# Scans of the next chunk ordered behind the masks of the present one on VectorE

## The chip, the cores and the metric

The kernel runs on one core of a Trainium2 chip. The metric is the time of one execution on the device in microseconds (us), the median of three runs. TensorE (PE) does the matrix products, VectorE (DVE), ScalarE (ACT) and GpSimd (POOL) the element-wise work, and SyncE (SP) issues all transfers from one queue. Each engine works through its own list of instructions in order and waits on semaphores.

## The reference

Three parts follow one another: a linear attention with decay, and two feed-forward layers.

```python
for t in range(S):                      # S = 768, for 4 batches and 8 heads of width 48
    state = alpha[:, :, t, :, None] * state + einsum('bhd,bhe->bhde', k[:, :, t], v[:, :, t])
    y[:, :, t] = einsum('bhd,bhde->bhe', q[:, :, t], state)
...
x = y as 3072 tokens x 384
h = x @ w_in;  x = (h * sigmoid(1.702 * h)) @ w_out      # 384 -> 2048 -> 384
h = x @ w_in2; x = (h - tanh(h)) @ w_out2
```

## The kernel before

The sequence of each batch is cut into six chunks of 128 tokens, so there are 24 chunks, counted here from 0. Within a chunk the recurrence becomes products. VectorE makes running products of the decays by two scans (`a_scan`: a memset of four columns, a scan, a reciprocal, a second scan). The keys and queries are scaled with them (`a_scale`, on GpSimd from chunk 8 on). TensorE makes the scores (`a_whole`, L298), VectorE masks them into SBUF in two halves (L301), and TensorE makes the output of a chunk in `a_out`: the queries times the carried state (L325) and the masked scores times the values (L332), both into the banks in which the scores were, and the chunk's own addition to the state (L341), which needs the keys turned by sixteen 32-row transposes on VectorE (`a_turn`, L308). `a_state` (L352, L353) then adds that to the state and multiplies it with the decays of the next chunk. `a_guard` (L254) squares the decays of a chunk in place on ScalarE, for a check at the end; the buffer of these decays is free for a load only after it. Results go to memory (`a_evac`: copies on ScalarE, L360, and four stores), come back turned (`a_back`, L378), and are split into a high and a low part (`a_x`: L382 on ScalarE, L383 on VectorE, the tile `xlo`). There are two sets of chunk buffers, so chunk g + 2 is loaded where chunk g was: the decays by L232, the keys by L234, the queries by L236, the values by L238.

The feed-forward layers run over six blocks of 512 tokens each, and over 16 slices m of the 2048 wide middle. Of each step TensorE makes nine products of the first kind (L392) and, three steps later, nine of the second (L399). In between ScalarE applies the function (L406) and rounds the result (L409, `ghi`), and VectorE makes the rest (L410, `glo`). `evac` (L442, L445) takes a finished block out. In the first layer's steps of block j the attention of the four chunks of block j + 1 is worked in small parts between the steps: `attend(g, r)` for the parts r = 0 to 3 of chunk g. Chunks 8 to 23 fall into blocks 1 to 4, some 135 to 450 us of the span; from chunk 8 (`FULL`) on a chunk's eight heads are worked at once. In blocks 2 and 3 weights are loaded a second time (L156) and checked on VectorE and ScalarE (`w_check`, L170 and L172), and towards the end of block 4 the second layer's weights are converted on VectorE (L163, L164, L176).

What sets the order: the lists of the engines are made by a scheduler of the language from the program, its dependencies and priorities. Only the first block's steps are held in the order written (`in_order`). After that the scheduler may move an instruction ahead of others that were written earlier, where no dependency forbids it. The masks carry a high priority. In the kernel before, the scans of chunk g + 1 are written ahead of the masks of chunk g.

Of the kernel before, what the change touches and what calls it, by code (L numbers as in the profile page):

```python
# [13 lines left out]
ALU = mybir.AluOpType  # L14
# [3 lines left out]
C = 128  # L18

FULL = 8  # L20
NCH = S // C
NG = B * NCH
NP = H // 2
# [45 lines left out]
def linear_attention_mlps(ctx, tc, xq, xv, fa, fv, cst, w1, w2, out):  # L69
    nc = tc.nc  # L70
    V, A, G, P, SP = nc.vector, nc.scalar, nc.gpsimd, nc.tensor, nc.sync
# [32 lines left out]
    ident, mask = cs[:, 0:128], cs[:, 128:256]  # L104
    seg = T("seg", (DP, AW))
    first = seg.rearrange("p (h t) -> p h t", h=NP)[:, :, 0:1]
# [92 lines left out]
    def src(g, n):  # L199
        return (third if g == 2 else late[(g + (g > 2)) % 2])[n][: DP if n < 4 else 128]  # L200

    def dec(g, n):
        return src(g, n)
# [4 lines left out]
    def dec3(g, n):  # L208
        return pairs(dec(g, n))


    def qq(g):
        return dec3(g, 2)

    def qkk(g):
        return dec3(g, 3)
# [20 lines left out]
        if 4 in parts:  # L237
            SP.dma_start(out=src(g, 4), in_=xv[g])  # L238

    def a_scan(g, n):  # L240
        if n == 0:
            V.memset(first, 1.0)
        V.tensor_tensor_scan(out=dec(g, n), data0=src(g, n), data1=seg, initial=0.0, op0=ALU.mult, op1=ALU.max)  # L243
        if n == 0:
            V.reciprocal(out=first, in_=dec3(g, 0)[:, :, C:])
# [26 lines left out]
    def a_scores(g, x, b):  # L272
        u = (2 * g + x) % 2
        q, k = qq(g), qkk(g)
        o = [bank[b + hh][:, : 2 * CE].rearrange("p (a t) -> p a t", a=2) for hh in range(2)]
        for i in range(2):
            for hh in range(2):
                r = slice(64 * hh, 64 * hh + D)
                P.matmul(out=o[hh][:, i], lhsT=k[r, 2 * x + i], rhs=q[r, 2 * x + i], start=True, stop=True)
        s4 = sm[u].rearrange("p (b a t) -> p b a t", b=2, a=2)  # L280
        kt = kts[u].rearrange("p (b a t) -> p b a t", b=2, a=2)
        for hh in range(2):
            A.copy(s4[:, hh], o[hh][:, :, :C])
        s3 = sm[u].rearrange("p (a t) -> p a t", a=4)
        G.affine_select(out=s3, in_=s3, pattern=[[0, 4], [1, C]], channel_multiplier=1, base=1 - C,
                        compare_op=ALU.is_ge, fill=0.0)
        for hh in range(2):
            A.copy(kt[:, hh], o[hh][:, :, C:])


    def a_whole(g, b):
        q, k = qq(g), qkk(g)
        s8 = sm8.rearrange("p (b a t) -> p b a t", b=2, a=NP)
        o = [bank[b + hh].rearrange("p (a t) -> p a t", a=NP) for hh in range(2)]
        for p in range(NP):
            for hh in range(2):
                r = slice(64 * hh, 64 * hh + D)
                P.matmul(out=o[hh][:, p], lhsT=k[r, p], rhs=q[r, p, :C], start=True, stop=True)  # L298
        for hh in range(2):
            with tc.high_priority():  # L300
                V.tensor_tensor(out=s8[:, hh], in0=o[hh], in1=mask.unsqueeze(1).to_broadcast([128, NP, C]), op=ALU.mult)  # L301

    def a_turn(g, low):
        k = pairs(late[(g + (g > 2)) % 2][3])
        for x in (0, 2) if low else (1, 3):
            d = kt8[g % 2][:, 4 * D * (x // 2) + 32 * (x % 2) :][:, : NP * D].rearrange("p (a d) -> p a d", a=NP)[:, :, :32]
            for y in range(4):
                V.transpose(out=d[32 * y : 32 * y + 32], in_=k[32 * x : 32 * x + 32, :, 32 * y : 32 * y + 32])  # L308
# [177 lines left out]
    def prep(g, part):  # L486
        if g >= NG:
            return
        if part < 2:
            a_scan(g, part)  # L490
        if part == 2:
            a_scale(g)
        if part == 3:
            a_guard(g)

    def a_done(g, b=5):
        a_evac(g, b)
        if g + 2 < NG:
            a_load(g + 2)
        if g < FULL:  # L500
            a_back(g)

    def attend(g, r, b=5):
        if r == 0:
            prep(g + 1, 0)
        if g < FULL and r < 2:
            a_scores(g, r, b)
        elif r == 0:
            if g == FULL:
                a_turn(g, 0)  # L510
            a_whole(g, b)
            a_turn(g, 1)
        if r == 2:
            a_out(g, b)
        if 0 < r < 3 or r == 3 and g >= FULL:
            prep(g + 1, r)
        if r == 3 and g >= FULL:
            a_done(g, b)
            if g + 1 < NG:
                a_turn(g + 1, 0)  # L520
# [69 lines left out]
    def place(s):  # L590
        l, j, m = steps[s]
        i = j if l == 1 else len(L1) + j
        t0, n = (L1 if l == 1 else L2)[j]
        alt = i >= len(L1) - 1 and (i - len(L1)) % 2
        return l, j, m, i, t0, n, [bank[b] for b in ((5, 6, 7) if alt else (0, 1, 2))]

    for s in range(NS + LAG):
        if s:
            if s <= NS:
                l, j, m, i, t0, n, acc = place(s - 1)  # L600
                prev = s - 1, n, V
        if s < NS:
            l, j, m, i, t0, n, acc = place(s)
# [13 lines left out]
        if s < NS:  # L617
            if l == 1 and j + 1 < len(L1):
                t1, n1 = L1[j + 1]
                if j:  # L620
                    parts, span = n1 // C * 4, 11
                    todo = range(min(parts, -(-m * parts // span)), min(parts, -(-(m + 1) * parts // span)))
                else:
                    todo = ((4 * (m // 3) + m % 3,) if m % 3 < 2 else (4 * (m // 3) + 2, 4 * (m // 3) + 3)) if m < 12 else ()
                for r in todo:
                    attend(t1 // C + r // 4, r % 4)
# [35 lines left out]
        if s >= LAG:  # L662
            l, j, m, i, t0, n, acc = place(s - LAG)
# [8 lines left out]
    with tc.If(bad != 0):  # L672
# [3 lines left out]
        for i in range(B * NP):  # L676
            b, p = divmod(i, NP)
# [96 lines left out]
```

## Time and profile before

| | |
|---|---|
| median of three runs | 953.47 us (952.26 to 953.66) |
| the profiled execution | 957.78 us, its span from first to last instruction 956.1 us |
| TensorE busy | 913.8 us, 96% of the span |
| VectorE busy | 676.5 us, 71% |
| ScalarE busy | 449.5 us, 47% |
| GpSimd busy | 85.9 us, 9% |
| mean granted clock of TensorE | 0.988 |

A busy TensorE here means that products follow one another without a gap; the end of a product is modelled. The busy share of the other engines says little, since each of them waits for TensorE most of the time. The idle time of an engine is listed with the instruction that ended it, as "[idle before <-what released it]".

### The profile page before, as it was taken

The numbers are of one execution on the slowest core, as the hardware profiler recorded it, in microseconds if no ns is written. First come the engines' busy times: TensorE is split into PE (matmuls) and PEld (weight loads), VectorE is DVE, ScalarE is ACT, GpSimd is POOL, SyncE is SP. The second block draws the span as 40 slices with busy tenths as digits, with TensorE's granted clock in tenths as the row PEclk, the third lists the DMA queues.
The fourth block names the chain that finished last, engine by engine and source line by source line (L and its number), as shares of the span: only waits on it lengthen the run. The fifth ranks groups of instructions, "written<-read, shape, count | busy, mean of one in ns | idle before, by whom it ended". The sixth has DMA issues, their size and how long they took to land.

```text
span 956.1 us, 13257 instructions
## 1 busy us (share of the span) xinstructions
PE 913.8 (96%) x4870; PEld 728.1 (76%) x4870; DVE 676.5 (71%) x1124; ACT 449.5 (47%) x906; POOL 85.9 (9%) x70
## 2 busy tenths in 40 slices
PE   5569999999989999999999999999999999999997
PEld 4347777777768777777888888888888888888885
DVE  7799997844774787484159986766776777766663
ACT  4445533323434434343344564554566566544542
POOL 1201211101120111110100200100100001000000
PEclk9999999989989999999999999999999999999999
DMA  9767434422643565434125410200322420000001
GB/s 268 236 201 240 137 87 125 120 68 79 200 132 141 159 196 198 128 113 158 32 93 181 138 60 1 78 22 1 113 96 89 166 99 1 33 1 1 34 1 37
DMA packets 58107, 101.91 MB, mean 107 GB/s; under 512 B 5024, under 2 KB 37408, under 8 KB 58032
## 3 DMA queue, kind: packets, MB, share of 16 engines
q1 hardware_dynamic: 58032, 100.97, 33.7%
q8 instruction: 40, 0.66, 0.3%
q14 instruction: 35, 0.29, 0.1%
HBM read 86.79 MB, written 14.16 MB: 106 GB/s over the span
## 4 chain that ended last, share of the span: by engine, by line
PE 61%; DVE 0%; issue 0%; ACT 0%; ACTq 0%
PE bank L399 30%; PE bank L392 29%; PE bank L332 1%; PE bank L298 0%; PE bank L325 0%; PE bank L341 0%; DVE xs L442 0%; DVE arena L301 0%; PE bank L268 0%; ACT xs L445 0%; ACTq L671 0%
## 5 line engine op out<-in xcount | busy, mean ns | idle before, releaser
L410 DVE TENSOR_TENSOR glo<-gt,ghi 128x512 fp32r<-128x512 f32 x192 | 140.1, 732 | 151.0 <-ACT ghi L409 146.8
L392 PE MATMUL bank<-xhi,whi 128*128 128x512 f32 x576 | 229.2, 398 | 9.5 <-ACT xhi L382 8.8
L399 PE MATMUL bank<-ghi,whi 128*128 128x512 f32 x576 | 233.1, 405 | 0.0
L399 PE MATMUL bank<-ghi,wlo 128*128 128x512 f32 x576 | 229.0, 397 | 0.0
L392 PE MATMUL bank<-xlo,whi 128*128 128x512 f32 x576 | 228.5, 397 | 0.4 <-DVE xlo L383 0.4
L399 PE MATMUL bank<-glo,whi 128*128 128x512 f32 x576 | 228.5, 397 | 0.0
L392 PE MATMUL bank<-xhi,wlo 128*128 128x512 f32 x576 | 228.1, 396 | 0.0
L409 ACT CAST ghi<-gt 128x512 fp32r<-128x512 f32 x192 | 119.2, 621 | 220.8 <-DVE gt L421 133.1
L392 PEld LDWEIGHTS bank<-xhi,whi 128*128 128x128 f32 x576 | 109.2, 190 | 35.6 <-ACT xhi L382 9.0
L399 PEld LDWEIGHTS bank<-ghi,whi 128*128 128x128 f32 x576 | 109.2, 190 | 28.4 <-issue 1.9
L392 PEld LDWEIGHTS bank<-xlo,whi 128*128 128x128 f32 x576 | 109.3, 190 | 26.4 <-DVE xlo L383 1.2
L399 PEld LDWEIGHTS bank<-glo,whi 128*128 128x128 f32 x576 | 109.4, 190 | 25.7
L392 PEld LDWEIGHTS bank<-xhi,wlo 128*128 128x128 f32 x576 | 109.1, 189 | 25.5
L399 PEld LDWEIGHTS bank<-ghi,wlo 128*128 128x128 f32 x576 | 109.5, 190 | 24.2 <-issue 0.5
L406 ACT ACTIVATE gt<-bank 128x512 f32<-128x512 f32 x96 | 57.4, 597 | 95.6 <-PE bank L392 72.0
L308 DVE STREAM_TRANSPOSE cf<-arena 32x128 f32<-32x128 f32 x256 | 77.5, 303 | 24.9 <-PE bank L341 10.0
L419 DVE SCALAR_TENSOR_TENSOR arena<-arena,bank 128x512 f32<-128x512 f32 x96 | 65.8, 686 | 29.4 <-ACT arena L417 28.6
L421 DVE SCALAR_TENSOR_TENSOR gt<-arena 128x512 f32<-128x512 f32 x96 | 68.3, 712 | 10.9 <-DVE arena L420 1.4
L417 ACT ACTIVATE arena<-bank 128x512 f32<-128x512 f32 x96 | 57.3, 597 | 36.1 <-PE bank L392 35.7
L243 DVE TENSOR_TENSOR_SCAN arena<-arena,seg 112x516 f32<-112x516 f32 x46 | 63.5, 1380 | 14.6 <-DMA arena<-xq 13.6
L418 ACT ACTIVATE arena<-arena,cs 128x512 f32<-128x512 f32 x96 | 69.6, 725 | 2.9
L420 DVE SCALAR_TENSOR_TENSOR arena<-arena 128x512 f32<-128x512 f32 x96 | 67.9, 707 | 3.0
(89 smaller groups left out, 663.2 us busy)
## 6 DMA issues: line engine op xcount, KB each, us to landing
raw<-w SPq DMA_DIRECT2D x64, 768.0 KB, 4.5
arena<-xq SPq DMA_DIRECT2D x46, 224.0 KB, 4.4
arena<-xq SPq DMA_DIRECT2D x22, 451.5 KB, 5.1
xlo<-xt SPq DMA_DIRECT2D x24, 192.0 KB, 4.4
x1t<-xs SPq DMA_DIRECT2D x6, 768.0 KB, 3.4
arena<-x1t SPq DMA_DIRECT2D x6, 768.0 KB, 4.5
out<-xs SPq DMA_DIRECT2D x18, 256.0 KB, 2.3
arena<-xv SPq DMA_DIRECT2D x23, 192.0 KB, 3.3
```

The costliest lines, as they stand in the source:

```text
L243: V.tensor_tensor_scan(out=dec(g, n), data0=src(g, n), data1=seg, initial=0.0, op0=ALU.mult, op1=ALU.max)
L308: V.transpose(out=d[32 * y : 32 * y + 32], in_=k[32 * x : 32 * x + 32, :, 32 * y : 32 * y + 32])
L392: P.matmul(out=h, lhsT=w[m][:, ws], rhs=x[:, k, :n], start=c == 0, stop=c == 3 * KT - 1)
L399: P.matmul(out=acc[k][:, :n], lhsT=w[m][:, ws], rhs=x[s % 3][:, :n], start=m == 0 and c == 0, stop=m == MT - 1 and c == 2)
L406: A.activation(out=gf[i][:, :n], in_=h, func=AF.Silu, scale=1.702)
L409: A.copy(ghi[s % 3][:, :n], gf[s % 2][:, :n])
L410: e.tensor_tensor(out=glo[s % 3][:, :n], in0=gf[s % 2][:, :n], in1=ghi[s % 3][:, :n].bitcast(F32), op=ALU.subtract)
L417: A.activation(out=u, in_=h, func=AF.Square, accum_out=usum[:, s - NS1 :][:, :1])
L418: A.activation(out=w, in_=u, func=AF.Square, bias=pbias)
L419: V.scalar_tensor_tensor(out=p, in0=u, scalar=P3, in1=h, op0=ALU.mult, op1=ALU.mult)
L420: V.scalar_tensor_tensor(out=p, in0=u, scalar=-PR, in1=p, op0=ALU.add, op1=ALU.mult)
L421: V.scalar_tensor_tensor(out=gf[i], in0=w, scalar=PD, in1=p, op0=ALU.add, op1=ALU.mult)
```

## The change

The scan of the next chunk is no longer called at the head of `attend` for chunks from 8 on. It is called after `a_whole`, and its first instruction, the memset, is ordered behind the second mask by a dependency that sets the order in the list and needs no semaphore, since both are on VectorE. For the chunks before 8 all stays as it was.

```diff
-    def a_scan(g, n):
+    def a_scan(g, n, after=None):
         if n == 0:
-            V.memset(first, 1.0)
+            ins = V.memset(first, 1.0).ins
+            if after:
+                tc.add_manual_dep(ins, after, mybir.DependencyInfo(
+                    mybir.DependencyClass.NoSync, mybir.DependencyReason.DATA), reason="masks")
         V.tensor_tensor_scan(out=dec(g, n), data0=src(g, n), data1=seg, initial=0.0, op0=ALU.mult, op1=ALU.max)
...
         for hh in range(2):
             with tc.high_priority():
-                V.tensor_tensor(out=s8[:, hh], in0=o[hh], in1=mask.unsqueeze(1).to_broadcast([128, NP, C]), op=ALU.mult)
+                last = V.tensor_tensor(out=s8[:, hh], in0=o[hh], in1=mask.unsqueeze(1).to_broadcast([128, NP, C]), op=ALU.mult)
+        return last.ins.name
...
     def attend(g, r, b=5):
-        if r == 0:
+        if r == 0 and g < FULL:
             prep(g + 1, 0)
         if g < FULL and r < 2:
             a_scores(g, r, b)
         elif r == 0:
             if g == FULL:
                 a_turn(g, 0)
-            a_whole(g, b)
+            masks = a_whole(g, b)
+            if g + 1 < NG:
+                a_scan(g + 1, 0, masks)
             a_turn(g, 1)
```

With the scans the scheduler moves other instructions too. The lines of the changed kernel are 3 to 6 higher: the masks are L304, the transposes L312, the state L356 and L357, `xlo` L387, the copy back L382, `glo` L414, `ghi` L413, the guard L257.

On VectorE, the rows up to chunk 11's masks in the kernel before (the scans of the chunks after it, L243, stand ahead of the two masks, L301):

```order
L308 STREAM_TRANSPOSE cf_100<-arena 32x4x32 x7
L410 TENSOR_TENSOR glo_112<-gt,ghi_109 128x512
L383 TENSOR_TENSOR xlo_105<-xlo_105,xhi_103 128x3x128
L410 TENSOR_TENSOR glo_113<-gt,ghi_110 128x512
L243 SCALAR_TENSOR_TENSOR arena<-arena,seg 112x516
L245 RECIPROCAL seg<-arena 112x4
L243 SCALAR_TENSOR_TENSOR arena<-arena,seg 112x516
L242 MEMSET seg 112x4
L243 SCALAR_TENSOR_TENSOR arena<-arena,seg 112x516
L301 TENSOR_TENSOR arena<-bank_128,cs 128x512
L301 TENSOR_TENSOR arena<-bank_129,cs 128x512
```

In the changed kernel, VectorE's rows around chunk 10's masks, from the transposes of chunk 10 to the first scan of chunk 11:

```order
L312 STREAM_TRANSPOSE cf_100<-arena 32x4x32 x16
L414 TENSOR_TENSOR glo_112<-gt,ghi_109 128x512
L356 TENSOR_TENSOR state<-bank_130,state 112x192
L357 TENSOR_TENSOR state<-state,arena 112x192
L414 TENSOR_TENSOR glo_113<-gt,ghi_110 128x512
L304 TENSOR_TENSOR arena<-bank_128,cs 128x512
L387 TENSOR_TENSOR xlo_105<-xlo_105,xhi_103 128x3x128
L304 TENSOR_TENSOR arena<-bank_129,cs 128x512
L242 MEMSET seg 112x4
L246 SCALAR_TENSOR_TENSOR arena<-arena,seg 112x516
```

The scans stand behind the masks, the transposes of a chunk stand between its scans and its masks and ahead of the state, and at this place the `xlo` of chunk 9 has come between the two masks of chunk 10.

On SP, in the kernel before, from the stores of chunk 9's result on (L365 the stores, L238 values, L378 the copy back, L232 decays, L234 keys):

```order
L365 DMA xt<-arena 48x2x128 x4
L238 DMA arena<-xv 128x384
L378 DMA xlo_105<-xt 128x3x128
L232 DMA arena<-xq 112x1032
L234 DMA arena<-xq 112x512
```

The same place in the changed kernel:

```order
L369 DMA xt<-arena 48x2x128 x4
L238 DMA arena<-xv 128x384
L232 DMA arena<-xq 112x1032
L382 DMA xlo_105<-xt 128x3x128
L234 DMA arena<-xq 112x512
```

The load of decays and the copy back have changed places; the same holds for chunks 8, 10 and 20. The third place is SP's list between the copy back of chunk 16 and the weight loads of the checks, in the changed kernel:

```order
L382 DMA xlo_105<-xt 128x3x128
L232 DMA arena<-xq 112x1032
L234 DMA arena<-xq 112x512
L453 DMA x1t<-xs 128x3x512
L232 DMA arena<-xq 112x1032
L236 DMA arena<-xq 112x4x128
L238 DMA arena<-xv 128x384
L369 DMA xt<-arena 48x2x128 x4
L156 DMA raw_96<-w 128x1536
L156 DMA raw_97<-w 128x1536
```

Before, both loads of decays (of chunks 19 and 20) stood together ahead of the load of keys, and the values ahead of the stores, as here. On ScalarE, the guard of a chunk stood behind the next `ghi` (chunks 9 and 10), and now stands ahead of it, directly behind the evacuation of the chunk before.

## Rows read from the trace of the kernel before

**Rows 1.** The page's first part: engine, busy us, share of span, instructions.
```profile
PE 913.8 (96%) x4870; PEld 728.1 (76%) x4870; DVE 676.5 (71%) x1124; ACT 449.5 (47%) x906; POOL 85.9 (9%) x70
```

**Rows 2.** TensorE's waits, 180 to 520 us: total, times, longest.
```profile
PE bank L325 <- DVE arena L301: 5.2, 5, 3.0
```

**Rows 3.** Timeline of TensorE: start, us, engine, line, operation [idle before <-releaser].
```profile
191.35 0.42 PE L325 MATMUL bank<-arena,state 48*48 48x128 f32 x4 [1.45 <-DVE arena L301]
191.95 1.09 PE L325 MATMUL bank<-arena,state 48*48 48x128 f32 x12 [0.18 <-DVE arena L301]
...
277.98 1.69 PE L325 MATMUL bank<-arena,state 48*48 48x128 f32 x16 [3.04 <-DVE arena L301]
```

**Rows 4.** Windows: us, busy PE PEld DVE ACT POOL, granted clock, DMA, GB/s.
```profile
191.80:198.60 6.80, 6.65 (x37) 5.14 (x38) 6.19 (x19) 1.36 (x3) 1.19 (x1) 0.51 0.38 100
277.10:283.90 6.80, 5.92 (x47) 4.70 (x48) 3.74 (x11) 0.74 (x2) 2.24 (x2) 0.51 0.22 57
```

**Rows 5.** Timeline of VectorE ahead of chunk 11's and chunk 15's masks.
```profile
188.45 2.27 DVE L243 TENSOR_TENSOR_SCAN arena<-arena,seg 112x516 f32<-112x516 f32 x1
190.64 1.26 DVE L301 TENSOR_TENSOR arena<-bank,cs 128x512 f32<-128x512 f32 x2
...
274.48 1.23 DVE L243 TENSOR_TENSOR_SCAN arena<-arena,seg 112x516 f32<-112x516 f32 x1 [1.52 <-DMA arena<-xq]
...
277.24 0.68 DVE L301 TENSOR_TENSOR arena<-bank,cs 128x512 f32<-128x512 f32 x1
```

**Rows 6.** Timeline of TensorE: scores of chunk 8, state products of 9 and 10.
```profile
139.20 1.16 PE L298 MATMUL bank<-arena 48*128 48x128 f32 x16
...
160.89 0.66 PE L325 MATMUL bank<-arena,state 48*48 48x128 f32 x16
...
173.01 0.66 PE L325 MATMUL bank<-arena,state 48*48 48x128 f32 x16
```

**Rows 7.** Timeline of VectorE, chunks 8 to 10: what its instructions take.
```profile
147.65 2.65 DVE L308 STREAM_TRANSPOSE cf<-arena 32x128 f32<-32x128 f32 x8
150.24 0.30 DVE L353 TENSOR_TENSOR state<-state,arena 112x192 f32<-112x192 f32 x1
...
152.91 0.69 DVE L410 TENSOR_TENSOR glo<-gt,ghi 128x512 fp32r<-128x512 f32 x1
...
157.55 0.67 DVE L442 TENSOR_SCALAR xs<-bank 128x512 f32<-128x512 f32 x1
...
174.06 2.24 DVE L243 TENSOR_TENSOR_SCAN arena<-arena,seg 112x516 f32<-112x516 f32 x1
```

**Rows 8.** Timeline of GpSimd beside the last of these.
```profile
174.03 1.18 POOL L249 TENSOR_TENSOR arena<-arena 112x512 f32<-112x512 f32 x1 [8.17 <-DVE seg L245]
```

**Rows 9.** Timeline of ScalarE: a cast of ghi, guard of 9, xhi of 8.
```profile
149.06 0.62 ACT L409 CAST ghi<-gt 128x512 fp32r<-128x512 f32 x1 [1.94 <-PE bank L399]
150.62 1.06 ACT L254 ACTIVATE arena<-arena 112x1032 f32<-112x1032 f32 x1 [0.95 <-DVE state L353]
...
153.73 0.51 ACT L382 CAST xhi<-xlo 128x384 fp32r<-128x384 f32 x1 [1.47 <-DMA xlo<-xt]
```

**Rows 10.** Timeline of SP: back8, and the pair of weight loads.
```profile
150.04 0.40 SPq L378 DMA_DIRECT2D xlo<-xt  x1
...
338.52 0.92 SPq L156 DMA_DIRECT2D raw<-w  x2
```

**Rows 11.** Line 378, the copies back: from issue to landing.
```profile
DMA to landing us min/median/max: 2.5/4.4/6.3
```

**Rows 12.** Timeline of TensorE: scores of chunk 17, output of chunk 18.
```profile
324.43 1.16 PE L298 MATMUL bank<-arena 48*128 48x128 f32 x16
...
346.63 0.43 PE L332 MATMUL bank<-arena 128*48 128x128 f32 x4 [0.21 <-DVE arena L301]
```

**Rows 13.** Timeline of VectorE: the weight check ahead of chunk 18's masks.
```profile
345.41 0.56 DVE L170 TENSOR_SCALAR wtb<-raw 128x768 int16<-128x768 int16 x1 [0.41 <-DMA raw<-w]
```

**Rows 14.** Groups of VectorE by line: a weight conversion, busy us, mean ns.
```profile
L164 DVE SCALAR_TENSOR_TENSOR cf<-raw,cf 128x768 int32<-128x768 int32 x22 | 21.4, 972 | 0.7
```

## The prediction, made before the changed kernel ran

> **What bounds the kernel now.** The page comes first: TensorE is busy for 96% of the span [rows 1], and the chain that ended last is almost wholly its two big products. So an edit that only reorders VectorE can give or take nothing but time in which TensorE stands, and time in which it runs at the lower clock. The table of TensorE's waits, asked for the stretch in which whole chunks are worked (180 to 520 us), has one line of weight: the product with the carried state (L325) waits for the mask (L301), 5.2 us in five waits [rows 2]. The timeline shows the two that matter: 1.45 and 0.18 us at 191 us (chunk 11) and 3.04 us at 278 us (chunk 15) [rows 3]. Each has a second cost. In the 6.8 us that follow, the granted clock is 0.51, which is the 1.2 GHz level, against 2.4 GHz around them [rows 4]. Work done at half rate loses half of the stretch: 3.4 us after the first; after the second 6.8 less the 0.88 us still idle, halved, 3.0 us. With a wait of 0.21 at chunk 18 [rows 12], what the order of masks costs now is 5.2 + 0.2 + 3.4 + 3.0 = 11.8 us.
>
> The cause is on VectorE's timeline: just ahead of the late masks stand scans of later chunks [rows 5]. One of them sat 1.52 us for its own transfer; another took 2.27 us; the masks behind them then began at 190.64 and 277.24 us although their scores had long been there.
>
> **What the change removes.** In the new order the masks of a chunk come ahead of the next chunk's memset and scans at all fifteen places, so these two waits lose their cause. What is left ahead of chunk 11's masks is glo and xlo; ahead of chunk 15's its own transposes, the state, two glo and an xlo, which by the chain worked below end about 1 us before the product is due. I book the whole 11.8 us as removed. No instruction is added or dropped; the memset carries an order, not a semaphore.
>
> **What it adds.** Before, scans, scaling and transposes of a chunk ran a chunk ahead. Now they form a loop from mask to mask, and it must fit in the 12 to 16 us between two chunks' scores. I work it out for chunks 8 to 10, on the times of before, since little ahead of chunk 8's scores changes but that VectorE has less to do.
>
> Scores of 8 begin at 139.2 and take 1.16 [rows 6]: 140.4. Two masks, 1.26 [rows 5]: 141.7. First scan 1.23 [rows 5], reciprocal 0.2, second scan 2.24 because GpSimd multiplies beside it [rows 7, 8]: 145.4. One glo, 0.65 (its row has 0.69 [rows 7] and overlaps the next a little): 146.1. Sixteen transposes, 5.3 (eight take 2.65 [rows 7]): 151.4. State, two instructions of about 0.33 [rows 7]: 152.1. Now ScalarE: its guard, which squares the decays in place, waits for that state, as it did before [rows 9], and ScalarE's cast of ghi now stands behind the guard: 1.07 + 0.62 [rows 9], 153.8. Then glo 0.65 and masks of 9, until 155.8; no harm, they are due at 160.9 [rows 6].
>
> But SP has changed too. The load of chunk 11's decays, which waits for that guard, now stands ahead of the copy back of chunk 8 (back8). Back8 was issued at 150.04 [rows 10]; now it is issued after 153.4, at about 153.9. These copies land 2.5 to 6.3 us after issue [rows 11]; before, this one took 3.7 [rows 9, 10]. I take 3.8, since 451 KB of decays now go out just ahead of it: 157.7. Cast and xlo, 0.5 each: 158.8. Chunk 10's scan stands behind this xlo: 1.23, evacuation 0.67, reciprocal, glo 0.65 and scan [rows 5, 7] end at 163; transposes 168.4; glo and state 169.8; guard 170.9; ghi and glo 172.2; first mask 172.9. Then the place that decides: xlo9 stands **between the two masks of chunk 10**. Its copy back again waits on SP for guard and load: issued 171.4, landed 175.2, cast and xlo 176.3, second mask 176.9. The product with the state was due at 173.0 [rows 6].
>
> The late evacuation costs TensorE first: the next column block's middle product needs it at about 159.5 (six matmuls of 0.23 ahead of the 160.9), and it ends near 160.7 or, with landings of 2.5, at 159.4: 0 to 1.2, I take 0.6. The wait for the second mask is then 2.0 with landings of 2.5, which bring every later step forward by 1.3, to 3.5 with those of 3.8 and no shift of TensorE; I take 2.6. Both ends lie above the 1.63 us after which the clock fell before [rows 3, 4], so a half-clock stretch follows, 3.3. Chunk 10: **6.5 us**.
>
> Chunk 18 is the second place. Chunk 17's scores begin at 324.43 [rows 12]; call it T. By the same loop chunk 17's masks end near T + 6.0 and chunk 18's second scan and a weight check near T + 11.1. The guard of 18 follows a check's sum on ScalarE, T + 13.2; the evacuation of chunk 17's result stands behind it, with a silu and a cast ahead: T + 15.1, four stores 1.8, and only then SP issues the pair of weight loads: T + 17.0. Before, they were issued at 338.52, T + 14.1 [rows 10]. The check that reads the first of them stands ahead of chunk 18's masks, and already got its data last, at 345.41 [rows 13], with TensorE waiting 0.21 for the mask [rows 12]. So about 2.9 more: a wait of 3.1. If the load, which took 6.9 us there, lands 2 us sooner because less is under way, it is 1.1. I take 2.5 and a half-clock stretch of 3.3: **5.8 us**.
>
> Chunks 20 to 23 repeat the pattern once more (load of decays ahead of the copy back): 0 to 1.2 us at the evacuation, 0.6. And ahead of chunk 23's masks stand eight weight conversions of up to 0.97 us [rows 14], 6 us that the scans now delay: 0 to 1.8, 0.9. Together **1.5 us**. Chunks 12 to 15, 16 and 19 come out with margins of about 1 us: nothing.
>
> **One rule beside it.** A scan took 1.23 us alone and 2.24 with GpSimd's multiply next to it [rows 5, 7, 8]. In the new order the scaling always begins right after the first scan, so it falls on the second scan or on the glo between. The Trainium skill (GPSIMD Engine Reference, Key points) says that GpSimd shares its SBUF interfaces with VectorE and that instructions with two SBUF inputs contend. By that rule every chunk's loop has this microsecond, and chunk 10's masks would come 1.0 later than in my chain, where the overlap is booked for chunk 9 alone; the sum would be 1 us higher.
>
> **The sum.** -11.8 + 6.5 + 5.8 + 1.5 = +2.0 us. The profiled execution took 957.78 us (span 956.1 and 1.7 around it), so 959.8; the median of the runs is 4.3 lower, 953.47, and there I forecast **955.5 us**. A measurement of this kernel can tell about 0.2% (1.9 us) from no change.
>
> **The rivals.**
> - *One new wait instead of two* (0.22). The pair of weight loads lands early, or the copies back land in 2.5. The profile speaks for it with the shortest landing [rows 11], against it with the check's late data [rows 13]. Without chunk 18's term but a wait of 1 us there: -11.8 + 6.5 + 1.0 + 1.5 = -2.8, so 950.7.
> - *Clean relief* (0.20), on the other side. TensorE never stands longer than it can without losing its clock. It decides at chunk 10: the second mask must end by 173.7 or so, which takes copies back that land in 2.5 and a loop about 1 us shorter than mine. Small waits of 3 us remain: -11.8 + 3 = -8.8, so 944.7. Against it: xlo9 between the masks.
> - *Worse* (0.18). The copies back land at their median of 4.4 or later [rows 11] because each follows a 451 KB load, and chunk 23's wait takes the clock as well: 0.9 more at chunk 10, 1.0 at the two evacuations, 3.3 for the clock: +2.0 + 5.2, so 960.7. The Trainium skill (DMA: Bandwidth & Descriptors, Queues, rings and completion order) says that each DMA engine takes descriptors in ring order; by that the copy back could hardly overtake the load, which points this way.
>
> **Numbers.** The forecast has 0.38, and its own bounds run from 953 to 958: 0.26 of it is slower by over 0.2%, 0.12 within. Worse adds 0.18 to slower. One wait runs from 949.5 to 953: 0.12 faster, 0.10 within. Clean relief is all faster; 0.02 is left for no effect. Faster 0.32, same 0.24, slower 0.44. The range from 946 to 961 leaves out most of the clean relief and the end of the worse case, some 2 in 10.
>
> **What would show it.** Right: no wait at chunks 11 and 15; L325 of chunk 10 waiting 2 us or more for L301, with xlo between the two masks waiting for ScalarE's cast and that for its transfer; a clock of 0.5 behind it; L332 of chunk 18 waiting, with the weight check ahead of the masks waiting for its load. Wrong: full clock from 100 us to the end, or new waits at chunks 12 to 15, where I found only a microsecond of margin.

## The result, and the profile after

The changed kernel takes 962.81 us, the median of five runs (960.93 to 963.17); the kernel before, run beside it, 953.47 us. The ratio is 1.0099 with a 95% interval of 1.0083 to 1.0114: it is 9.3 us slower. The forecast of 955.5 us was too low, and the time lies outside its range (946 to 961). The profiled execution of the changed kernel took 963.17 us (span 961.1), close to the median, whereas that of before had been 4.3 us above its median.

The table of TensorE's waits between 130 and 520 us, asked of the changed kernel (us in total, times, longest):

```profile
PE bank L329 <- DVE arena L304: 3.7, 1, 3.7
PE bank L329 <- DVE seg L242: 2.7, 2, 2.5
PE bank L403 <- ACT xs L449: 1.8, 2, 1.0
PE bank L396 <- ACT gt L410: 1.4, 1, 1.4
PE bank L336 <- DVE arena L304: 0.9, 1, 0.9
PE bank L336 <- DVE seg L242: 0.2, 1, 0.2
```

In place of the waits of [rows 2] there are 10.7 us of waits, in new places. "DVE seg L242" is the memset that follows the masks on VectorE; it is named because its semaphore came last, and the mask is what was late. On TensorE's timeline:

```profile
158.61 0.50 PE L403 MATMUL bank<-ghi,whi 128*128 128x512 f32 x1 [0.85 <-ACT xs L449]
...
177.30 1.09 PE L329 MATMUL bank<-arena,state 48*48 48x128 f32 x10 [2.54 <-DVE seg L242]
...
213.37 0.50 PE L396 MATMUL bank<-xhi,whi 128*128 128x512 f32 x1 [1.38 <-ACT gt L410]
...
277.91 0.65 PE L329 MATMUL bank<-arena,state 48*48 48x128 f32 x16
...
344.38 0.43 PE L336 MATMUL bank<-arena 128*48 128x128 f32 x4 [0.89 <-DVE arena L304]
...
448.45 1.69 PE L329 MATMUL bank<-arena,state 48*48 48x128 f32 x16 [3.66 <-DVE arena L304]
```

The row at 277.91 is chunk 15's product, which before waited 3.04 us [rows 3]; it now starts without a wait. Chunk 10 (177 us) waits 2.54, chunk 18 (344 us) about 1.1, chunk 23 (448 us) 3.66. The windows, with the granted clock ahead of the last two numbers:

```profile
177.20:180.60 3.40, 3.30 (x36) 2.89 (x36) 3.32 (x6) 0.66 (x2) 1.62 (x1) 0.51 0.25 66
446.90:453.70 6.80, 5.25 (x36) 3.86 (x37) 3.56 (x5) 1.18 (x3) 0.00 (x0) 0.50 0.48 151
191.80:198.60 6.80, 6.51 (x52) 4.71 (x51) 4.53 (x8) 2.65 (x5) 0.72 (x1) 1.00 0.20 60
277.10:283.90 6.80, 6.80 (x69) 5.38 (x68) 6.42 (x14) 1.24 (x3) 2.69 (x2) 1.00 0.49 115
```

Both half-clock stretches of [rows 4] are gone, and there are two others: 3.4 us long after chunk 10's wait, 6.8 us long at chunk 23.

**Where the time went, place by place.** For every profiled execution of this study, this table gives the time from the start of one chunk's scores to that of another's (the first row of the line in `a_whole` on TensorE's timeline), in us. "End" is the end of the span. A wait and the half-clock stretch behind it show up in one column.

| kernel | 9 to 11 | 11 to 12 | 14 to 15 | 15 to 16 | 17 to 19 | 19 to 20 | 20 to 23 | 23 to end |
|---|---|---|---|---|---|---|---|---|
| before | 32.21 | 41.72 | 16.13 | 43.32 | 32.24 | 38.15 | 44.23 | 517.05 |
| before again (e1) | 32.21 | 38.65 | 16.13 | 40.66 | 31.91 | 40.40 | 44.24 | 516.97 |
| changed | 38.66 | 38.96 | 16.13 | 37.23 | 33.13 | 37.20 | 46.13 | 523.25 |
| e2, block 1 | 38.34 | 43.44 | 16.13 | 43.47 | 31.94 | 37.95 | 44.23 | 516.65 |
| e3, block 4 | 32.20 | 37.55 | 16.14 | 43.19 | 32.80 | 37.24 | 46.12 | 526.24 |
| e4, blocks 2, 3 | 32.21 | 36.65 | 16.13 | 37.24 | 33.29 | 43.02 | 44.23 | 516.85 |
| e5, copy first | 32.74 | 36.66 | 18.21 | 38.49 | 33.41 | 38.35 | 44.78 | 525.79 |
| e6, conversion | 38.41 | 38.89 | 16.14 | 37.23 | 33.10 | 37.17 | 46.09 | 517.92 |
| e7, both | 32.73 | 36.66 | 20.31 | 37.11 | 35.46 | 37.12 | 44.76 | 518.86 |
| e8, and guard | 32.74 | 36.66 | 17.54 | 39.13 | 32.13 | 38.56 | 44.78 | 520.85 |
| e9, blocks 2, 3 | 32.20 | 36.66 | 16.76 | 38.19 | 33.19 | 40.77 | 44.23 | 518.88 |
| e10, block 2 | 32.20 | 36.65 | 16.13 | 40.32 | 32.32 | 37.88 | 44.20 | 518.86 |

Changed against before, the columns give +6.45 (chunk 10), -2.76 (chunk 11's wait, less a new one), -6.09 (chunk 15), +0.89 (chunk 18), -0.95, +1.90 (evacuation at chunk 21) and +6.20 (chunk 23): +5.6, and with 0.64 won ahead of chunk 9 the 5.0 us by which the spans differ. That is 4.3 us less than the medians say. The columns of before and of before taken again show why: 11 to 12 and 15 to 16 differ by 3.07 and 2.66 us between two executions of one program, 19 to 20 by 2.25 the other way, and the spans by 3.4.

### The profile page after: what moved, and what is told of

Its sections match the earlier page's. It is cut to its first block, busy times and chain, and to the rows that moved or that the text cites. A ratio compares the mean times of both kernels' runs of the same rounds, so it can differ in the third digit from the quotient of the medians.

```text
span 961.1 us, 13246 instructions
## 1 busy us (share of the span) xinstructions
PE 913.7 (95%) x4870; PEld 726.6 (76%) x4870; DVE 678.4 (71%) x1124; ACT 446.4 (46%) x906; POOL 89.5 (9%) x70
## 4 chain that ended last, share of the span: by engine, by line
PE 59%; DVE 2%; DMA 1%; issue 1%; ACT 0%; SPq 0%; ACTq 0%
PE bank L403 30%; PE bank L396 28%; DMA raw<-w 1%; DVE cf L312 1%; PE bank L336 0%; DMA xlo<-xt 0%; PE bank L301 0%; DVE arena L304 0%; PE bank L329 0%; DVE arena L246 0%; DVE cf L164 0%; DVE glo L414 0%; DVE xs L446 0%; PE bank L345 0%; ACT gt L410 0%
## 5 line engine op out<-in xcount | busy, mean ns | idle before, releaser
L414 DVE TENSOR_TENSOR glo<-gt,ghi 128x512 fp32r<-128x512 f32 x192 | 140.4, 732 | 163.3 <-ACT ghi L413 159.5
L413 ACT CAST ghi<-gt 128x512 fp32r<-128x512 f32 x192 | 119.0, 620 | 190.5 <-DVE gt L425 130.8
L312 DVE STREAM_TRANSPOSE cf<-arena 32x128 f32<-32x128 f32 x256 | 77.5, 303 | 8.0
L246 DVE TENSOR_TENSOR_SCAN arena<-arena,seg 112x516 f32<-112x516 f32 x46 | 66.7, 1449 | 3.8 <-DMA arena<-xq 2.7
```

Source lines behind the costliest of these rows:

```text
L413: A.copy(ghi[s % 3][:, :n], gf[s % 2][:, :n])
L414: e.tensor_tensor(out=glo[s % 3][:, :n], in0=gf[s % 2][:, :n], in1=ghi[s % 3][:, :n].bitcast(F32), op=ALU.subtract)
```

## The experiments

Theory A: the waits that the changed kernel's own profile shows are the loss, made by what moved with the scans (copy back behind a load on SP, a conversion ahead of masks), and the removed term was sized from an execution that held more of it than the ordinary one. The rivals: B, that the removed term is right in every execution and the changed kernel loses 4 us unseen; C, that the scans' place costs a little at each chunk; D, that the loop from mask to mask is itself too long, or a relieved wait only lets the next one come.

**e1: the kernel before, once more.** No edit. 

> The kernel before once more, unchanged. Theory A (the removed term was sized from one execution that was 4.3 us slower than the median, and ordinary executions hold less of these waits): its profile shows less than 5.2 us of waits of the state product (L325) for the mask, or fewer half-clock stretches than the two of 6.8 us, and waits plus half-clock loss come to some 6 to 7 us rather than 11.8. Theory B (the removed term was right, and the changed kernel loses some 4 us more than the waits in its own profile show): again 5.2 us of waits and two stretches of 6.8 us, in an execution near 953.5 us.

Measured: 951.63 us, ratio 0.9989 (0.9968 to 1.0011); the profiled execution took 954.41 us, 2.8 above that median. Its waits at chunks 11, 15 and 19:

```profile
191.83 0.42 PE L325 MATMUL bank<-arena,state 48*48 48x128 f32 x4 [1.45 <-DVE arena L301]
...
275.10 0.42 PE L325 MATMUL bank<-arena,state 48*48 48x128 f32 x2 [2.77 <-DVE arena L301]
...
357.99 0.42 PE L325 MATMUL bank<-arena,state 48*48 48x128 f32 x2 [1.04 <-DVE arena L301]
```

and the windows behind them:

```profile
191.60:198.40 6.80, 6.39 (x51) 4.98 (x52) 6.25 (x18) 1.87 (x4) 1.19 (x1) 1.00 0.49 125
275.20:282.00 6.80, 6.62 (x61) 5.32 (x62) 5.08 (x15) 1.94 (x4) 1.28 (x2) 1.00 0.45 119
359.20:362.60 3.40, 3.40 (x32) 3.12 (x30) 1.08 (x4) 0.74 (x2) 0.47 (x1) 0.52 0.34 94
```

The waits are nearly those of [rows 3], 1.45 and 2.77 us (5.8 us in all with that of 1.04 us at chunk 19), which speaks against A's first guess. But the clock stayed at 1.00 behind both, and fell behind the one of 1.04 us. So B falls, and A is right in the second of its guesses: the waits come in both executions and the fall of the clock does not. Of the booked 11.8 us, 6.4 hung on that. Waits plus clock here are 5.8 + 0.2 + 1.7 = 7.7 us, more than the 6 to 7 that A expected; by the columns of the table, as they are read for the kernel before below, it is 8.6.

Two profiles are few, but the mean granted clock was measured in every run. The profiled execution of before, with its two stretches, had 0.988, and e1's, with one short stretch, 0.993. The kernel before ran 77 times more beside the experiments. In 30 of these runs the mean was 0.991 or more, which leaves no room for both stretches: 11 with at least 0.993 have a median of 950.4 us, 19 with 0.991 or 0.992 one of 952.9. Four with 0.989 or 0.990 took 953.5 to 959.6 us, and the one with 0.988 took 957.75, as long as the profiled execution. In the other 42 the mean can't tell, since it is also lower where the clock is low at the start (last section). So the half clock differs from execution to execution, and the time with it by about as much as the prediction's 4.3 us.

**e2: scans behind the masks for chunks 8 to 11 alone.**

```diff
+    def behind(g):
+        return g in range(8, 12)
...
-        if r == 0 and g < FULL:
+        if r == 0 and not behind(g):
             prep(g + 1, 0)
...
-            if g + 1 < NG:
+            if behind(g) and g + 1 < NG:
                 a_scan(g + 1, 0, masks)
```

> Scans behind the masks for chunks 8 to 11 alone; the rest as before. Theory A: at chunk 10 the waits of the changed kernel return (0.85 us for the evacuation at 158 us, 2.5 us for the second mask at 177 us, 1.7 us for the clock, 1.4 us at 213 us), 6.5 us in all, and before's wait at chunk 11 with its clock goes, 3 to 5 us; so 955 to 957 us, ratio 1.002 to 1.004. Rival C (the loss of the changed kernel is made by the scans' place in every block, a little at each chunk): a quarter of 9.3, 955.8 us, and no wait of over 1 us at chunk 10.

Measured: 962.71 us, ratio 1.0102 (1.0071 to 1.0134), above both expectations. Chunk 10's wait came back (2.59 us; 9 to 11 takes 38.34), so C falls. The rest came from the border between the two orders, where scans and transposes of two chunks, 12 and 13, stand ahead of a glo (the row at 212 us):

```profile
212.28 0.79 PE L403 MATMUL bank<-glo,whi 128*128 128x512 f32 x1 [3.14 <-DVE glo L414]
...
284.91 1.48 PE L329 MATMUL bank<-arena,state 48*48 48x128 f32 x13 [3.61 <-DVE arena L304]
```

with a half-clock stretch of 6.8 us at each. The second row is chunk 15's old wait.

**e3: the same for chunks 20 to 23 alone** (`range(20, 24)`). 

> Scans behind the masks for chunks 20 to 23 alone; the rest as before. Theory A: the wait of 3.7 us at chunk 23 with its half-clock stretch (3.4 us) and 1.0 us for the evacuation come back, 8.1 us, and nothing is removed: 961.6 us, ratio 1.0085. If the wait at chunk 23 needs the lateness from the blocks ahead, or the loss is spread evenly (rival C): 955.8 us or less, ratio below 1.0025.

Measured: 960.70 us, ratio 1.0087 (1.0063 to 1.0112), as A expected. Chunk 23 waits 3.74 us, with 6.8 us at half clock behind, and the evacuation at 410 us 0.96; from chunk 20 to 23 it takes the 46.1 us of the changed kernel. The last column has 3.0 us more than there: 1.9 are of another cause (the last section), and the half-clock stretch here began behind the wait, while in the changed kernel its first 1.5 us lay in the wait. So block 4's loss owes nothing to the blocks ahead of it.

This run shows one thing more. From chunk 8 up to chunk 11's masks the engines' lists are those of the kernel before, and yet the masks cost TensorE 0.4 us there and not 1.6. VectorE's last scan ahead of these masks, GpSimd's multiplication beside it, and TensorE:

```profile
188.45 1.23 DVE L246 TENSOR_TENSOR_SCAN arena<-arena,seg 112x516 f32<-112x516 f32 x1
...
188.71 1.96 POOL L252 TENSOR_TENSOR arena<-arena 112x512 f32<-112x512 f32 x1 [10.63 <-DMA arena<-xq]
...
190.32 0.42 PE L329 MATMUL bank<-arena,state 48*48 48x128 f32 x4 [0.23 <-DVE arena L304]
```

Here the scan began 0.26 us ahead of the multiplication and took 1.23 us, the multiplication 1.96. In the kernel before the multiplication began 0.02 us ahead (188.43 against 188.45) and took 1.20, the scan 2.27 [rows 5]. So the wait itself, and not only the clock behind it, differs between executions of the same order.

**e4: chunks 12 to 19 alone** (`range(12, 20)`). 

> Scans behind the masks for chunks 12 to 19 alone (blocks 2 and 3); chunks 8 to 11 and 20 to 23 as before. Theory A: the waits at chunks 11 and 15 are gone (no later scan stands ahead of those masks), none of the new ones at chunks 10 and 23 come, some 1 us at chunk 18 stays: 953.5 - 6.5 + 1 = 948 us, ratio 0.994. Theory B: 953.5 - 11.8 + 1 = 942.7 us, ratio 0.989. Rival C: 953.5 + 4.6 = 958 us.

Measured: 954.09 us, ratio 1.0013 (0.9991 to 1.0034), which is none of the three times expected. The waits at chunks 11 and 15 are gone (36.65 and 37.24 us), none came at 10 and 23, and up to chunk 19 this execution is 10.7 us ahead of before's and 5.1 ahead of e1's. At the border of the orders 5.8 us are lost again (19 to 20). TensorE, and below it ScalarE and VectorE there:

```profile
368.43 0.79 PE L396 MATMUL bank<-xhi,whi 128*128 128x512 f32 x1 [4.03 <-ACT gt L410]
...
366.74 1.06 ACT L257 ACTIVATE arena<-arena 112x1032 f32<-112x1032 f32 x1 [10.26 <-DVE state L357]
...
363.88 1.23 DVE L246 TENSOR_TENSOR_SCAN arena<-arena,seg 112x516 f32<-112x516 f32 x1
365.15 0.65 DVE L312 STREAM_TRANSPOSE cf<-arena 32x128 f32<-32x128 f32 x2
365.83 0.81 DVE L357 TENSOR_TENSOR state<-state,arena 112x192 f32<-112x192 f32 x1
```

Two chunks' scans and transposes stand ahead of the state; the guard waits for the state, the silu stands behind the guard, and TensorE waits for the silu.

**e5: the changed kernel with the copy back first on SP.**

```diff
-            SP.dma_start(out=t[:DP, : 2 * AW], in_=xq[g, :, : 2 * AW])
+            ald = SP.dma_start(out=t[:DP, : 2 * AW], in_=xq[g, :, : 2 * AW])
+            if after:
+                tc.add_manual_dep(ald.ins, after, mybir.DependencyInfo(
+                    mybir.DependencyClass.NoSync, mybir.DependencyReason.DATA), reason="back")
...
-        a_evac(g, b)
+        bk = a_evac(g, b)
         if g + 2 < NG:
-            a_load(g + 2)
+            a_load(g + 2, after=bk)
```

> The changed kernel, with the copy back of a chunk ordered ahead of the next load of decays on SP, as it stood before. If the exchange on SP makes the waits (theory A): the waits at 158 us (0.85), at chunk 10 (2.5, with 1.7 for the clock) and at chunk 21 go, 6.4 + 1.9 us, so 962.8 - 8.3 = 954.5 us, ratio 1.002; the wait at chunk 23 stays. If the loop from mask to mask is itself too long (theory D, scans and transposes of a chunk no longer fit): chunk 10's second mask stays 2 us late or more and the time stays at 960 us or above.

Measured: 957.11 us, ratio 1.0043 (1.0029 to 1.0058), so 5.7 us less than the changed kernel where 8.3 were expected. SP's and VectorE's rows for chunks 9 and 10 (the copy back is L386 here, xlo L391, the masks L307):

```profile
165.69 0.40 SPq L386 DMA_DIRECT2D xlo<-xt  x1
...
169.55 0.56 DVE L391 TENSOR_TENSOR xlo<-xlo,xhi 128x384 fp32r<-128x384 f32 x1 [0.20 <-ACT xhi L390]
170.03 1.28 DVE L307 TENSOR_TENSOR arena<-bank,cs 128x512 f32<-128x512 f32 x2
```

The copy back is issued 5.7 us earlier than in the changed kernel, xlo is done ahead of both masks, and chunk 10's wait is gone (32.74 us). So is the wait at 213 us (11 to 12 takes 36.66): it was a consequence of chunk 10's late masks. The exchange on SP is what made them late, not the length of the loop; with the copy back the scheduler also moved the xlo of chunks 8, 9 and 20 ahead on VectorE, and what each of the two moves does alone was not run. Chunk 23's wait stays, as expected (3.16 us). But 2.1 us are lost at chunk 14, and chunk 18 waits 1.7, which the next but one run explains, and two silus cost 0.95 and 0.96 us (284 and 368 us).

**e6: the changed kernel with one conversion behind chunk 23's masks.**

```diff
+        if l == 2 and m == 3:
+            tc.add_manual_dep(ins, final[0], mybir.DependencyInfo(
+                mybir.DependencyClass.NoSync, mybir.DependencyReason.DATA), reason="masks")
```

(`ins` is that conversion's first instruction in `w_bits`, `final[0]` the last mask.) 

> The changed kernel, with one weight conversion (its two instructions that wait for a load) ordered behind chunk 23's masks on VectorE; nothing else moves. If the load that this conversion waits for makes chunk 23's wait (theory A): the wait of 3.7 us and its half-clock stretch go, 962.8 - 6.1 = 956.7 us, ratio 1.004. If the scans' delay alone makes it (theory D): the mask still ends after the product is due, over 1 us of wait, 960 to 963 us.

Measured: 957.62 us, ratio 1.0048 (1.0029 to 1.0066), as A expected. VectorE now (masks L308):

```profile
442.24 1.28 DVE L308 TENSOR_TENSOR arena<-bank,cs 128x512 f32<-128x512 f32 x2
444.54 0.56 DVE L164 TENSOR_SCALAR arena<-raw 128x768 int32<-128x768 int32 x1 [1.02 <-DMA raw<-w]
```

and in the changed kernel:

```profile
446.24 0.56 DVE L163 TENSOR_SCALAR arena<-raw 128x768 int32<-128x768 int32 x1 [2.26 <-DMA raw<-w]
446.84 0.96 DVE L164 SCALAR_TENSOR_TENSOR arena<-raw,arena 128x768 int32<-128x768 int32 x1
447.71 1.28 DVE L304 TENSOR_TENSOR arena<-bank,cs 128x512 f32<-128x512 f32 x2
```

A conversion that waited for its own transfer held the masks. The product's wait fell from 3.66 to 0.5 us in two parts and the clock did not fall.

**e7: both edits.** 

> Both edits of the two runs before this one: copy back first on SP, the conversion behind chunk 23's masks. Theory A: 962.8 - 8.3 - 6.1 = 948.4 us, ratio 0.9955, so faster than the kernel before; what is left is some 2 us at 213 us and 1 us at chunk 18. Theory D: not below 956 us.

Measured: 953.83 us, ratio 1.0004 (0.9988 to 1.0020): no difference from before that can be told, and not the 948.4 expected. What was to go is gone but for 0.5 us at each of the two evacuations, and two other waits stand there, at chunks 14 and 18 (20.31 and 35.46 us in the table). VectorE ahead of those masks (weight check L174, masks L311):

```profile
253.14 0.56 DVE L174 TENSOR_SCALAR wtb<-raw 128x768 int16<-128x768 int16 x1 [1.46 <-DMA raw<-w]
253.62 1.28 DVE L311 TENSOR_TENSOR arena<-bank,cs 128x512 f32<-128x512 f32 x2
...
338.56 0.56 DVE L174 TENSOR_SCALAR wtb<-raw 128x768 int16<-128x768 int16 x1 [5.04 <-DMA raw<-w]
339.03 1.28 DVE L311 TENSOR_TENSOR arena<-bank,cs 128x512 f32<-128x512 f32 x2
```

TensorE waited 1.96 and 2.21 us for them, each with 3.4 us at half clock behind. D's time (not below 956) was not met either, but D is right in this much: with SP's order put back, the weight checks ahead of the masks become the late ones.

**e8: both edits, and the guard behind the evacuation copies on ScalarE** (the same kind of order, from the copies of chunk g to the guard of g + 1). 

> Both edits, and the guard of the next chunk ordered behind the evacuation copies on ScalarE. If the guard ahead of chunk 11's evacuation makes the late silu at 213 us: 2.3 us less than with both edits alone, 946 us, ratio 0.993; if the cast behind the copy back is late for another reason: the same as with both.

Measured: 953.03 us, ratio 0.9995 (0.9980 to 1.0010). From 11 to 12 it takes 36.66 us with and without the guard's move, so that edit is worth nothing at the place for which it was made; e5 had already taken the wait. Elsewhere the waits moved: in the two profiled executions 14 to 15 and 17 to 19 fell by 2.8 and 3.3 us, and 15 to 16 and 19 to 20 rose by 2.0 and 1.4. The difference of 0.8 us to e7's median lies inside both spreads.

**e9: chunks 12 to 19, with the scan of chunk 21 behind the state of chunk 19.**

```diff
-            prep(g + 1, 0)
+            a_scan(g + 1, 0, done[0] if g == 20 else None) if g + 1 < NG else None
```

(The line is shown against e4; `done[0]` is the last multiplication of the state.) 

> Scans behind the masks for chunks 12 to 19 as in e4, and the scan of chunk 21, which there stood ahead of chunk 19's state, ordered behind that state. If the two scans and 16 transposes more ahead of the state made e4's late guard and so its silu wait of 4.0 us with 1.7 for the clock, 5.7 us go: 954.1 - 5.7 = 948.4 us, ratio 0.995, faster than both kernels. If relief of one wait only lets the next one come (theory D): 952 to 955 us, ratio 0.999 to 1.002.

Measured: 951.76 us, ratio 0.9983 (0.9967 to 1.0000). The wait of 4.03 us is gone; in its place stand three smaller ones (1.04, 0.54 and 1.14 us between 373 and 382 us), so 19 to 20 fell from 43.02 to 40.77 and not to 37.2. The two scans ahead of the state did make the wait, but the time is nearer to D's than to the 948.4 of A: most of what one relief gives, other waits take.

**e10: chunks 12 to 15, with the scan of chunk 17 behind the state of chunk 15.** The same edit for `range(12, 16)` and `g == 16`. 

> Scans behind the masks for chunks 12 to 15 alone, the scan of chunk 17 ordered behind the state of chunk 15; the rest as before. It removes the waits at chunks 11 and 15 only and adds none that the order shows: what an ordinary execution holds of these two waits, 4.5 us for the waits alone by the profile of before taken again plus the clock in some executions, so 948 us, ratio 0.994 to 0.995; with 11.8 us, as booked in the prediction, 942 us, ratio 0.988.

Measured: 950.24 us, ratio 0.9969 (0.9951 to 0.9986). This one beats both kernels, by 2.8 us against before run beside it (953.08), though by less than the 0.994 to 0.995 expected. Its waits between 285 and 305 us, where the orders meet, sum to 2.3 us:

```profile
291.23 0.50 PE L404 MATMUL bank<-glo,whi 128*128 128x512 f32 x1 [0.66 <-DVE glo L415]
293.67 0.50 PE L397 MATMUL bank<-xhi,whi 128*128 128x512 f32 x1 [0.54 <-ACT gt L411]
299.26 0.50 PE L397 MATMUL bank<-xhi,whi 128*128 128x512 f32 x1 [1.14 <-ACT gt L411]
```

Gain and new waits together are 5.1 us, or 5.9 if the border is taken from the table (15 to 16 takes 40.32 us here and 37.23 in the changed kernel). That is an estimate of what the two old waits are worth in the ordinary execution; it mixes a median with one profile, and the interval of the ratio alone leaves 1.7 us either way. It is a little more than their 4.5 us of standing, and far from 11.8.

## Why the prediction missed

It said +2.0 us between profiled executions and took 4.3 off for the median. Between profiled executions it was +5.4 (963.17 less 957.78), at the median +9.3. So 3.4 us of the miss of 7.3 are in the terms and 4.0 in the step to the median (the changed kernel's profiled execution lay 0.4, not 4.3, above its median).

**The step to the median failed first.** "The median of the runs is 4.3 lower" was used as if the excess of that execution had nothing to do with the change. It had: e1 shows nearly the same waits without the two falls of the clock, and 30 of 77 other runs have a mean clock too high for both. The 11.8 us were rightly read off one execution: from 11 to 12 it lies 5.07 us above the 36.65 that are reached without a wait, and from 15 to 16 and from 19 to 20 6.09 and 0.95 above the changed kernel, 12.1 in all. But 6.4 of them were two falls of the clock that come in some executions and not in others. An ordinary execution gives back some 5 to 9 us, by estimate: 5.1 to 5.9 by e10, 7.7 by the waits and the clock of e1, 8.6 by its columns.

**Chunk 10, 6.5 us: the mechanism right, the size 6.45 by two errors that cancelled.** The chain held to a few tenths on the clock of the trace. Forecast and measured: masks of chunk 8 end 141.7 and 141.0, back8 issued 153.9 and 153.24, back9 171.4 and 171.39, second mask ended 176.9 and 177.2. The rows:

```profile
170.88 0.33 SPq L232 DMA_DIRECT2D arena<-xq  x1
171.39 0.39 SPq L382 DMA_DIRECT2D xlo<-xt  x1
...
175.54 0.51 ACT L386 CAST xhi<-xlo 128x384 fp32r<-128x384 f32 x1 [3.68 <-DMA xlo<-xt]
...
176.08 0.56 DVE L387 TENSOR_TENSOR xlo<-xlo,xhi 128x384 fp32r<-128x384 f32 x1 [3.39 <-ACT xhi L386]
176.56 0.68 DVE L304 TENSOR_TENSOR arena<-bank,cs 128x512 f32<-128x512 f32 x1
```

xlo9 stands between the masks, waits for the cast, and that for its transfer, as forecast. Chunk 8's scores began at 138.57 and not 139.20, so counted from them the second mask came 0.97 us later than forecast; 0.85 of that are the two copies back, which were used 4.30 and 4.15 us after their issue where 3.8 had been taken. The parts of the 6.45 were off in two directions: the scores of chunks 9, 10 and 11 start at 150.59, 168.35 and 189.25 us, so the late evacuation took 1.76 where 0.6 was booked (its row shows 0.85 as idle; the ends of matmuls are modelled), and chunk 10's wait with its clock 4.69 where it was 5.9, since the stretch is 3.4 us long and not 6.8. That the two cancel is luck. Two sentences from the Trainium skill stood beside this chain. By the one on the interfaces that GpSimd shares with VectorE (the Trainium skill, GPSIMD Engine Reference, Key points) chunk 10's masks should have come 1.0 later than the chain; they came 0.3 later by the clock of the trace, and counted from chunk 8's scores the copies back explain most of the 0.97, so this number does not test the rule. The trace agrees with it in kind: chunk 10's second scan took 1.22 us, but the glo ahead of it, beside GpSimd's multiplication, 1.36 in place of 0.69. By the one on ring order (the Trainium skill, DMA: Bandwidth & Descriptors, Queues, rings and completion order) the copy back should hardly overtake the load. The 4.30 and 4.15 us fit that, but copies of this line landed after 2.5 to 6.3 us before the change too [rows 11], so no run here tests it.

**A knock-on that the prediction did not follow: 2.3 us at 213 us.** Chunk 10's late masks delayed what follows them on VectorE and with it the scaling of chunk 12, for which that chunk's guard waited 5.73 us on ScalarE. Chunk 11's evacuation, stores and copy back stand behind the guard, and a silu behind the cast. In e5 they stand in the same order, the guard waits 3.04 us, and TensorE doesn't wait:

```profile
201.82 1.07 ACT L257 ACTIVATE arena<-arena 112x1032 f32<-112x1032 f32 x1 [5.73 <-POOL arena L253]
...
202.89 0.63 ACT L364 COPY arena<-bank 112x256 f32<-112x256 f32 x2
...
212.31 0.51 ACT L386 CAST xhi<-xlo 128x384 fp32r<-128x384 f32 x1 [7.12 <-DMA xlo<-xt]
212.72 0.59 ACT L410 ACTIVATE gt<-bank 128x512 f32<-128x512 f32 x1
```

The chain was worked out to chunk 10's second mask and not beyond.

**Chunk 18, 5.8 us: the mechanism right, the size not, 0.9.** The weight check ahead of the masks waits for its load, as forecast:

```profile
343.17 0.56 DVE L170 TENSOR_SCALAR wtb<-raw 128x768 int16<-128x768 int16 x1 [4.49 <-DMA raw<-w]
343.64 1.28 DVE L304 TENSOR_TENSOR arena<-bank,cs 128x512 f32<-128x512 f32 x2
```

With chunk 17's scores at 321.39, the pair of loads was issued at T + 16.1 (337.52) and not T + 17.0, and the check had its data 5.65 us later where 6.9 had been taken. So the two terms that were mis-sized are the issue (0.9 us too late; chunk 17's masks ended at T + 5.4 where 6.0 had been taken) and the landing (1.25 too long). The wait was 1.06 us, and the clock held. In e7, where the loads went out at T + 17.8, the same place cost 2.21 us and a fall of the clock.

**Chunk 23, 0.9 us: the step that failed worst, 6.2.** The eight conversions ahead of the masks were counted by the time that they take. One of them also waits for a load, which SP can issue only when an earlier conversion has freed its buffer. That was at 441.91 us, and the data came at 446.2 (the rows are with e6). The scans had pushed the conversions together, and the transfer came to lie ahead of the last two of them and of the masks behind these. The trace of before held the fact: there the same load was issued at 435.06, and the conversion waited for it too, but early enough:

```profile
439.62 0.56 DVE L163 TENSOR_SCALAR arena<-raw 128x768 int32<-128x768 int32 x1 [0.74 <-DMA raw<-w]
```

The first question for an instruction ahead of a mask is what it waits for, and here it was not asked. With the evacuation at chunk 21 (1.9 us, 0.6 forecast), chunks 20 to 23 cost 8.1 instead of 1.5.

In sum, against the forecast's terms: chunk 23 +5.3, the evacuation +1.3, the knock-on +2.3, chunk 18 -4.9, the removed term -0.3 and nothing at chunk 10: +3.7, beside the 3.4 above (0.6 us were won ahead of chunk 9, and 0.4 lie outside the spans). The rival "worse" (960.7) had the right sign and, with a clock that falls at chunk 23, one of the right causes.

## What to carry to other kernels

A wait read from one profiled execution is one sample: its standing time can differ in the next (chunk 11 in e3), the fall of the clock behind it is to be booked by its chance, and when the execution lies above the median, the excess is first looked for in the very term that the change removes. When a scheduler is given one new order, read every instruction that now stands ahead of the critical one for what it waits for, a transfer above all: here a copy back, a weight check and a conversion, each waiting for its own transfer ahead of critical work, made most of the new waits. A change that is good in one stage and bad in its neighbours can be made in that stage alone (e10, 0.3% faster), but the border between the two orders is a new place to look.

## What the runs showed of the hardware

- The same wait does not always bring the half-clock stretch. Waits of 1.45 and 3.04 us had it in the first execution of before; 1.45 and 2.77 had none in the second, and there 1.04 had one. Behind the wait of 2.77 us in e3 there is one. The prediction had taken every wait above 1.63 us to bring it. The window behind e3's wait:

```profile
273.30:280.10 6.80, 6.41 (x48) 5.09 (x49) 3.72 (x11) 0.74 (x2) 1.76 (x2) 0.50 0.23 63
```

- The stretch is either 3.4 us long (after chunk 10's wait in the changed kernel, e2 and e6, in e4 behind 4.03 us, in e7) or 6.8 us long (before, chunk 23 in the changed kernel), and the longer wait does not always have the longer one. What decides both is open.
- A scan of VectorE beside a multiplication of GpSimd: the one that began first kept its time, and the other took longer (scan 2.27 and multiplication 1.20 us in the kernel before, 1.23 and 1.96 in e3). The spans of GpSimd are rough.
- The mean granted clock of an execution says little about the waits unless the start is known. In some executions TensorE runs at 0.50 from 20 to 55 us, where it waits for transfers in any case: from 25 to 30 us the granted clock is 0.50 in the changed kernel and 1.00 in the kernel before, with TensorE busy for 3.72 and 3.65 us. Chunk 8's scores nevertheless begin at 138.57 us with the low clock and 139.20 without.
- In the profiled executions of e3, e5, e8, e9 and e10 the products behind the attention take 1.9 us longer than in the others, at a granted clock of 1.00 and without waits: from VectorE's evacuation of block 4 to that of the last block 465.22 us (e8, 477.02 to 942.24) against 463.38 (e7, 479.91 to 943.29). What follows the last evacuation by VectorE takes 6.9 to 8.9 us. Neither was followed up; both stand in the table's last column, and profiled executions can differ by them without any wait.
